# Fewer transposes on TensorE, and the order of a hand-planned attention and MLP kernel searched anew

## The chip, the cores and the metric

The kernel runs on one core of one Trainium2 chip. The metric is device time in microseconds (us), as a median of runs. TensorE (PE) multiplies, VectorE (DVE) and ScalarE (ACT) work element by element and take results out of PSUM, GpSimd (POOL) here issues the loads that change float32 into bfloat16, and SyncE (SP) issues DMA transposes and stores.

## The reference

Attention without softmax and with a decay per head, then an MLP with exact GELU over all tokens:

```
q, k, v: (8, 8, 576, 64)                       # batch, heads, sequence, head size
gamma = 1 - 2 ** (-5 - head)
D[i, j] = gamma ** (i - j) if i >= j else 0
attn = ((q @ k.T) / 8 * D) @ v                 # per batch and head
x = attn as (4608, 512)                        # tokens, heads * head size
out = gelu(x @ w_in) @ w_out                   # w_in (512, 2048), w_out (2048, 512)
```

## The kernel before

**Units, pairs and blocks.** The sequence of 576 is cut into chunks of 128 (the last, a tail, has 64). A unit is 128 tokens: one chunk of one batch entry, or the tails of two. There are 36 units. Batch entries go two by two; a pair is the same chunk of two entries. Units 0 to 3 (two pairs) come first, then 4 and 5, 6 and 7, 8 and 9 (the fifth pair), the tail 10, 11 and 12, and so on. Four units make a block of 512 tokens for the MLP, and there are nine blocks, t = 0 to 8.

**Attention of a unit.** q, k and v land in bfloat16. Then q and k are turned, so that the head size lies on partitions: for units below `N_PE_TR` by TensorE (`turn`, four products against the identity for q and four for k, into the PSUM tile `qk_ps`, copied to `qkT` by `turned_copy` on VectorE or ScalarE), for the others by one DMA transpose for q and one for k of a whole pair, issued on SP (`turn_dma`, L613). `scores` multiplies k with q (PSUM tile `sc`), VectorE multiplies by the decay (L657, `ret`), `inner` multiplies by v (`o_ps`), and `cross` adds what older chunks leave in a state `u`, which `state` collects in `u_ps` from k and the scaled values `vh`. `vh` of a unit is one VectorE instruction, or eight ScalarE instructions where the unit is in `VH_ACT` (L829). The result is copied or scaled into `xT` of its block.

**MLP of a block.** The first product (`hT`) is followed by a GELU on ScalarE. For blocks 0 and 1 it is plain: block 1 in two halves of 256 tokens; in block 0 the eight pairs of 128 hidden columns that `WIDE` lists are multiplied with 512 tokens at once, after those that it does not list, which are multiplied with 128 tokens (one unit) at a time, as `CUTS` has it:

```
if t == 0: cuts of 128 tokens, m in K_ORDER[::2] if m not in WIDE
then       [("1", t, m + n, 1, 0, TOK) for m in WIDE for n in range(2)]
```

The pieces of that second list run in the order of the list. From block 2 on, groups of hidden columns are either plain ("p3") or go by a fast scheme of seven products ("units" `yT`, `zT`, `xT_`, with sums `xs` of x and `wi_sum` of the weights). `LAYOUTS` says which group of a block goes how and in which order; "01" weaves the products of two groups, "0", "1" runs them one after the other, "2p3" weaves a fast with a plain one. The second product (`oT`) is plain for block 0 and fast from block 1 on, in the order `SECOND`; results go to `o_sb` and are stored from SP, the last block's from ScalarE's queue as well.

**What sets the order.** While the program is built, a planner with an estimated length for every operation simulates the engines and emits instructions in the order in which they would start. The order on each engine is thus fixed in the built program, and each engine runs its own in order. Loads are issued on GpSimd in the sequence `ORDER` (q1 is q of unit 1; wi3 and wo3 are the fourth of eight pieces of w_in and w_out; `pos` is a small table), at most eight in flight, from unit 11 on in the order of the units, with four buffers for pairs. Attention's products are put between the MLP's as short stretches; `need`, made of `LEAD` and `SPREAD`, and `SHIFT`, `APART`, `BEFORE`, `GAP_A`, `HOLD`, `LOOK` and `EASE` set when and in which grouping. In its first 16 us the planner fills each pause of TensorE with products of zeros (`warm`), 512 columns wide or 128, that nobody reads.

Of the kernel before, what the change touches and what calls it, by code (L numbers as in the profile page):

```python
# [29 lines left out]
class Plan:  # L30
# [9 lines left out]
    def add(self, name, engine, dur, deps, fn, due=0.0, lag=0.12, **more):  # L40
        assert name not in self.ops, name
        op = self.ops[name] = Op(name, engine, dur, deps, fn, due, lag, **more)
        for d in op.deps:
            if d.startswith("land"):
                self.users.setdefault(d, []).append(op)
            dep = self.ops.get(d)
            if dep is None or dep.end is None:
                op.waits += 1
                self.later.setdefault(d, []).append(op)
            else:  # L50
                op.ready = max(op.ready, dep.end + dep.lag)
        if not op.waits:
            self.released(op)
        return op
# [53 lines left out]
def kernel(  # L108
# [47 lines left out]
    def pair_with(i):  # L156

        bp, ci, j = units[i]
        return [i] if j is None else pair_of[bp, ci]

    def slot_of(i):
        return pair_with(i)[0]
# [2 lines left out]
    n = v_order.index(pair_of[1, 1][0])  # L165
    v_order[n:n] = kept

    N_PE_TR = 10
    N_LD = 4
    N_QKT = 4  # L170
    N_VH = 5
    N_RET = 3
    N_Q = 4
    VH_ACT = [5, 6, 7, 8, 9, 10, 21, 22, 23, 24, 26, 27, 28, 29, 30, 31, 33, 34, 35]
    HOT = 10.1
    N_WARM = 8
    SLACK = 0.2
    CUTS = (0, 128, 256, 384, 512)
    AHEAD = 6
    WIDE = [2, 10, 14, 12, 4]  # L180
    VH_DUE = 14.0
    PARTS = 4
    FAST = 1
    FETCH = 4.0
    BUSY_FETCH = 6.2
    GAP_A = 4.7
    GAP_B = 0
    SHIFT = {4: -0.5, 5: 4.0, 6: 4.5, 7: -2.0, 8: 6.0, 9: 0.5, 10: 0.5, 11: -6.0, 12: -3.5, 13: -0.5, 14: -3.5, 15: -0.5, 16: -4.5, 17: -2.0, 18: -3.5, 19: 0.0, 20: 1.0}
    APART = [3, 5, 6, 7]
    BEFORE = 8.1  # L190
    UNIT_FROM = 2
    LOOK = 12
    HOLD = 6
    LAYOUTS = {2: ['01', '2', 'p3'], 3: ['01', '2', 'p3'], 4: ['1', '02', 'p3'], 5: ['0', '1', '2', 'p3'], 6: ['01', '23'], 7: ['01', '23'], 8: ['0', '12', 'p3']}
    LEAD = 8.9
    SPREAD = 5.6
    EASE = 9
    ORDER = ("k2 k1 pos q1 wi0 q3 k3 q2 v1 v2 v3 wi4 wi7 wi1 wi5 v4 k4 q5 wi6 k5 wi3 wi2 q4 wo0 v5 wo4 wo1 q9 wo5 "
             "q8 v7 wo6 v6 q7 q6 wo2 k7 v10 wo7 wo3 k6 q10 k8 v8 k10 k9 v9").split()
    K_ORDER = [0, 1, 8, 9, 2, 3, 10, 11, 4, 5, 12, 13, 6, 7, 14, 15]  # L200
    PRODUCTS = "3251467"
    SECOND = "1267534"
# [1 line left out]
    for t in range(UNIT_FROM, N_BLK):  # L204
        LAYOUT[t] = LAYOUTS[t]

# [99 lines left out]
    for t in range(N_BLK):  # L306
        if t < 2:
            cuts = CUTS if t == 0 else (0, 256, 512)
            for lo, hi in zip(cuts, cuts[1:]):
                stream.append([("1", t, m, 2, lo, hi) for m in K_ORDER[::2] if t or m not in WIDE])  # L310
            if t == 0:
                stream.append([("1", t, m + n, 1, 0, TOK) for m in WIDE for n in range(2)])
        else:
# [44 lines left out]
    pos = const.tile([128, 1, NCI], FP32, name="pos")  # L358
# [121 lines left out]
    def tiles_of(i):  # L480

        if i not in loaded:
            n = slot_of(i)
            if i in kept:
                loaded[i] = (const.tile([128, 2, H, D], BF16, name=f"qk_ld{i}"), const.tile([128, H, D], BF16, name=f"v_ld{i}"))
                return loaded[i]
            if n not in slots:
                ld_ring.take()
                slots[n] = (ld_pool.tile([128, 2, H, 2, D], BF16, tag="qk", name="qk_ld"),
                            ld_pool.tile([128, 2, H, D], BF16, tag="v", name="v_ld"))  # L490
            qk, v_ld = slots[n]
            j = units[i][2] or 0
            if i in old:
                loaded[i] = (qk.rearrange("p a (j h) b d -> p j a (h b) d", j=2)[:, j], v_ld[:, j])
            else:
                loaded[i] = (qk[:, :, :, j], v_ld[:, j])
        return loaded[i]

    def read(i, what):
# [4 lines left out]
        want = {(m, x) for m in pair_with(i) for x in  # L504
                ["v"] + (["turn0", "turn1"] if i < N_PE_TR else ["turn"]) + (["state"] if units[i][1] < NCI - 1 else []) + (["inner"] if i in raw else [])}
        if i not in kept and want <= got:
# [33 lines left out]
    for i in range(11, N_U):  # L540
        ORDER += [f"{what}{i}" for what in "qkv"]
    prev = ["val"]
    for item in ORDER:
        what = item.rstrip("0123456789")
# [77 lines left out]
    def scores(i):  # L622
        if i in old:
            qkT = qkT_of(i)
            got = [bank([128, HP, 128], FP32, f"sc{e}") for e in range(2)]
            for hp in range(HP):
                for e in range(2):
                    sl = slice(64 * e, 64 * e + 64)
                    product(got[e][1][:, hp, :], lhsT=qkT[sl, 1, hp, :], rhs=qkT[sl, 0, hp, :],
                                     start=True, stop=True)  # L630
        else:
            qkT, n = qkT_of(i), i - slot_of(i)
            got = [bank([128, HP, 128], FP32, f"sc{e}") for e in range(2)]
            for hh in range(HP):
                h = 4 * n + hh
                for half in range(2):
                    out_ = slice(64 * half, 64 * half + 64)
                    for e in range(2):
                        sl = slice(64 * e, 64 * e + 64)
                        product(got[e][1][out_, hh, :], lhsT=qkT[sl, 1, h, out_], rhs=qkT[sl, 0, h, :],  # L640
                                         start=True, stop=True)
        st[i]["sc"] = got
# [225 lines left out]
    for n, g in enumerate(groups):  # L868
        need[n] = begins["1", g[0] // 4] - LEAD
    for n in reversed(range(len(groups) - 1)):  # L870
        need[n] = min(need[n], need[n + 1] - SPREAD)
    tiles_of(0)
# [5 lines left out]
    EARLY = 3  # L878
    ALONE = [groups[n][0] for n in range(2, len(groups)) if n in APART or groups[n - 1][0] not in fine]
    for i in range(N_U):  # L880
# [4 lines left out]
        room_T = lambda i=i: 0.0 if slot_of(i) in turned_of else tr_ring.at()  # L885
        if i < N_PE_TR:
            for jj, nm in enumerate("qk"):
# [7 lines left out]
        if i not in fine and i not in tails:  # L895
            add(f"scores{i}", "pe", 0.23, [f"T{i}.0", f"T{i}.1"] if i < N_PE_TR else [f"landT{m}" for m in duo],
                lambda i=i: scores(i), due, DRAIN, banks=2, mode="row" if i in old else "quad")
# [16 lines left out]
        if i > n:  # L914
            continue
        Ts = [f"T{m}.{jj}" for m in duo for jj in range(2)] if n < N_PE_TR else [f"landT{m}" for m in duo]
        if n in ALONE:
# [15 lines left out]
    for i in v_order:  # L933
        due = need[group_of[i]] + 3.0 if i not in kept else need[group_of[pair_of[1, 1][0]]] - 2.0
        n = v_order.index(i)
        room = lambda i=i, due=due: max(0.0 if "vh" in st[i] else vh_ring.at(), due - EASE if group_of[i] > 3 else 0.0)
        before = ["dv", f"land v{i}"] + ([f"vh{v_order[n - 1]}"] if n else [])
        if i in VH_ACT:
            step_ = H // PARTS
# [472 lines left out]
    def macro_of(n):  # L1412


        back, front = groups[n - 1], groups[n] if n < len(groups) and n not in APART else []
        states = states_behind(n - 1)
# [12 lines left out]
    def scores_of(front):  # L1429
        return [f"both_{i}" if i in fine or i in tails else f"scores{i}" for i in front if i not in fine or i == slot_of(i)]  # L1430

    def states_behind(n):

        if n < 0:
            return []
        i = groups[n][0]
        bp, ci, j = units[i]
        if j is None:
            return [(1, 0)] if bp == 0 else []
        return [] if (bp, ci) == (1, 0) else [(bp, ci)]  # L1440
# [3 lines left out]
    for n in range(EARLY + 1, len(groups) + 1):  # L1444
        macros += [(n, names, need[n - 1] + SHIFT[n]) for names in macro_of(n)]
        if n in APART:
            macros.append((n, scores_of(groups[n]), need[n] - BEFORE))
    in_macro = {nm for m in macros for nm in m[1]}
# [98 lines left out]
    def pe_candidates():  # L1547
# [7 lines left out]
        if macros and not got:  # L1555
            ahead = next((W[r[0]] for r in heads if r), NEVER)
            n, ops, due = macros[0]
            hold = ahead >= due + HOLD and (macro_start(ops, False) or NEVER) <= T["pe"] + 0.3
        for run in heads:
# [4 lines left out]
            else:  # L1564
                look = run[:LOOK]
            for one in look:
# [7 lines left out]
        if macros and not any(g[1] == 0 for g in got):  # L1574
            n, ops, due = macros[0]
            at = macro_start(ops)
            if at is not None:
                at = max(at, stretch_end[0] + (GAP_B if ops[0].startswith("in_b") else GAP_A))
                ahead = next((W[r[0]] for r in heads if r), NEVER)
# [10 lines left out]
    while True:  # L1590
# [12 lines left out]
        if e == "pe":  # L1603
# [9 lines left out]
            else:  # L1613
                for run in heads:
                    got = [one for one in run[:LOOK] if f"mlp{one}" == op.name]
                    if got:
# [46 lines left out]
```

## Time and profile before

| | us |
|---|---|
| median of 3 runs | 280.59 (280.51 to 280.66) |
| the profiled execution | 281.12 |
| its span, first to last instruction | 279.2 |
| TensorE busy | 273.0 (98%), 3626 products |
| VectorE, ScalarE, GpSimd busy | 228.7, 181.7, 110.4 |
| granted TensorE clock | 1.000 |

The profile is of one execution. Matmuls are pipelined and their ends are modelled, so busy TensorE time says little; the distance from the start of one product to that of the next says what it costs. A landing is the time at which the last part of a DMA's data has arrived.

### The profile page before, as it was taken

Reading aid. Unit: us, or ns where it says so; the run is one execution under the profiler, and the core shown is the slowest. Engines: PE = TensorE matmul, PEld = TensorE weight load, DVE = VectorE, ACT = ScalarE, POOL = GpSimd, SP = SyncE. Lnnn points to the kernel's source line nnn. Section 1 sums busy time; section 2 is a strip of 40 time slices with the busy share of each in tenths; the row PEclk is TensorE's granted clock in tenths of the full one; section 3 lists DMA queues with packets and bytes.
Section 4 is the critical chain, followed back from the end, with each engine's and each line's share of the span. In section 5 each row is a group of like instructions: output and inputs, shape, how many; then the busy total and the mean of one; then the engine's idle time right before and its main releaser. Section 6 shows DMA issues by size and latency. Waiting matters only on the chain.

```text
span 279.2 us, 8727 instructions
## 1 busy us (share of the span) xinstructions
PE 273.0 (98%) x3626; PEld 216.2 (77%) x3626; DVE 228.7 (82%) x437; ACT 181.7 (65%) x446; POOL 110.4 (40%) x139
## 2 busy tenths in 40 slices
PE   7999999999999999999999999999999999999995
PEld 2675567478888688868886888778888888888684
DVE  5862554589989997999898999997899979969843
ACT  7766638786418823693559657975896689627840
POOL 8977688809755097311452725705000000000000
PEclk9999999999999999999999999999999999999999
DMA  9999999999999999999999999999600040003013
GB/s 150 161 187 179 190 175 173 178 169 165 149 142 177 193 134 151 134 236 99 142 197 88 128 160 222 116 113 121 190 2 2 6 151 2 2 22 131 0 40 113
DMA packets 152374, 35.55 MB, mean 127 GB/s; under 512 B 141072, under 2 KB 148240, under 8 KB 152336
## 3 DMA queue, kind: packets, MB, share of 16 engines
q0 software_dynamic: 115792, 17.97, 97.6%
q1 hardware_dynamic: 34544, 15.93, 31.0%
q10 hardware_dynamic: 2000, 1.11, 1.4%
q8 instruction: 28, 0.46, 0.7%
q14 instruction: 10, 0.08, 0.1%
HBM read 36.70 MB, written 9.44 MB: 165 GB/s over the span
## 4 chain that ended last, share of the span: by engine, by line
PE 79%; DMA 14%; POOL 5%; issue 1%; ACT 0%; DVE 0%; POOLq 0%
PE oT L231 37%; PE zT L231 11%; PE hT L231 9%; DMA w_out<-in_moe_w_out_dram 9%; PE yT L231 7%; PE o_ps L231 4%; DMA w_in<-in_moe_w_in_dram 3%; PE sc L231 2%; POOL qk_ld L522 2%; DMA qk_ld<-in_k_dram 2%; PE u_ps L231 2%; POOL w_in L528 1%; POOL v_ld L522 1%; PE xT__1851 L231 0%; PE xT__5150 L231 0%
## 5 line engine op out<-in xcount | busy, mean ns | idle before, releaser
L231 PEld LDWEIGHTS <-g 128*128 128x128 bf16 x576 | 55.2, 98 | 12.5 <-issue 0.4
L231 PEld LDWEIGHTS <-w_in 128*128 128x128 bf16 x528 | 47.2, 98 | 15.9
L231 PEld LDWEIGHTS <-wi_sum 128*128 128x128 bf16 x460 | 44.6, 98 | 7.1 <-issue 0.4
L231 PE MATMUL hT<-xT,w_in 128*128 128x256 bf16 (+2 forms) x344 | 49.0, 295 | 0.0
L231 PE MATMUL oT<-w_out,g 128*128 128x256 bf16 (+1 forms) x320 | 45.6, 294 | 0.1
L522 POOL DMA_DIRECT2D qk_ld<-in_q_dram x31 | 27.8, 898 | 38.9 <-DMA qkT<-qk_ld 24.2
L829 ACT ACTIVATE vh<-v_ld,dv 128x64 bf16<-128x64 bf16 x152 | 41.3, 348 | 1.0 <-DVE ret L657 1.0
L231 PEld LDWEIGHTS <-s 128*128 128x128 bf16 x384 | 36.8, 98 | 5.3 <-issue 0.4
L1104 ACT ACTIVATE g<-hT 128x512 bf16<-128x512 f32 (+1 forms) x58 | 31.5, 558 | 11.1 <-PE hT L231 10.4
L522 POOL DMA_DIRECT2D v_ld<-in_v_dram x31 | 28.0, 906 | 14.0 <-issue 6.7
L231 PE MATMUL oT<-w_sum,s 128*128 128x256 bf16 x256 | 32.6, 273 | 0.3 <-issue 0.3
L231 PE MATMUL oT<-w_sum,g 128*128 128x256 bf16 x256 | 31.1, 273 | 0.0
L1248 ACT COPY o_sb<-oT 128x512 f32<-128x512 f32 (+1 forms) x27 | 14.3, 539 | 23.7 <-PE oT L231 12.1
L522 POOL DMA_DIRECT2D qk_ld<-in_k_dram x31 | 28.0, 905 | 2.8 <-DMA v_ld<-in_v_dram 1.4
L1217 ACT ACTIVATE g<-zT 128x512 bf16<-128x512 f32 x46 | 26.4, 608 | 0.7 <-DVE zT L1226 0.6
L657 DVE TENSOR_TENSOR ret<-sc,msk 128x512 bf16<-128x512 f32 x36 | 22.9, 683 | 4.3 <-PE sc L231 4.3
L1252 DVE TENSOR_TENSOR o_sb<-o_sb,oT 128x512 f32<-128x512 f32 (+1 forms) x27 | 16.6, 626 | 10.5 <-PE oT L231 5.7
L834 ACT CAST u_sb<-u_ps 128x512 bf16<-128x512 f32 x19 | 11.3, 596 | 14.4 <-PE u_ps L231 12.5
L860 DVE TENSOR_TENSOR xT<-o_ps,dqT 128x512 bf16<-128x512 f32 x26 | 17.1, 683 | 1.9 <-PE o_ps L231 1.9
L573 DVE COPY qkT<-qk_ps 128x512 bf16<-128x512 bf16 x16 | 6.4, 421 | 13.9 <-PE qk_ps L235 13.8
L1226 DVE TENSOR_TENSOR zT<-q,zT 128x512 f32<-128x512 f32 x23 | 15.8, 692 | 2.1 <-PE zT L231 1.8
L575 ACT COPY q<-yT 128x512 f32<-128x512 f32 x16 | 9.0, 600 | 11.7 <-PE yT L231 11.7
(173 smaller groups left out, 470.6 us busy)
## 6 DMA issues: line engine op xcount, KB each, us to landing
out_dram<-o_sb SPq DMA_DIRECT2D x29, 256.0 KB, 3.4
qk_ld<-in_k_dram POOLq DMA_DIRECT2D x31, 128.0 KB, 7.2
qk_ld<-in_q_dram POOLq DMA_DIRECT2D x31, 128.0 KB, 7.5
v_ld<-in_v_dram POOLq DMA_DIRECT2D x31, 128.0 KB, 7.8
w_in<-in_moe_w_in_dram POOLq DMA_DIRECT2D x8, 256.0 KB, 8.1
w_out<-in_moe_w_out_dram POOLq DMA_DIRECT2D x8, 256.0 KB, 8.4
out_dram<-o_sb SPq DMA_DIRECT2D x7, 128.0 KB, 2.4
out_dram<-o_sb ACTq DMA_DIRECT2D x5, 128.0 KB, 1.9
```

The source lines that it names most:

```text
L231: return nc.tensor.matmul(*args, **more)
L522: nc.gpsimd.dma_start(dst, src[2 * bp + j, :, ci * C:ci * C + C, :].rearrange("h s d -> s h d"))
L575: nc.scalar.copy(dst, src)
L657: nc.vector.tensor_tensor(r, t, by, op=ALU.mult)
L829: nc.scalar.activation(vh[:, h], loaded[i][1][:, h], AF.Copy, scale=dv[:, h, ci:ci + 1])
L834: ins = (nc.vector.tensor_copy if engine == "dve" else nc.scalar.copy)(u_sb[t if bp >= FINE else ci % 2], u_bank[1])
L860: nc.vector.tensor_tensor(dst, o, dqT[:, :, ci * C:ci * C + C], op=ALU.mult)
L1104: nc.scalar.activation(g_of(t, m0)[:, m0 % 2:m0 % 2 + n, m0 // 8, lo:hi], hT, AF.Gelu)
L1217: nc.scalar.activation(target(key, what), chain[key][n][1], AF.Gelu)
L1226: nc.vector.tensor_tensor(to, chain[key]["q"], z, op=ALU.add)
L1248: nc.scalar.copy(target(key, what), chain[key][n][1])
L1252: nc.vector.tensor_tensor(to, to, chain[key][n][1], op=ALU.add)
```

## The change

`N_PE_TR` goes from 10 to 8, so units 8 and 9 are turned by two DMA transposes on SP and no longer by 16 products on TensorE with four copies. `WIDE` lists all eight pairs of block 0, so nothing of it is multiplied by units any more. `VH_ACT` gives 14 units to ScalarE where it gave 19 (36 and 37 are no units). The loads have a new `ORDER`, blocks 3, 5, 6, 7 and 8 a new layout, and several constants and the shifts of the planner's placing are others. No line of a function changes.

```
-    N_PE_TR = 10
+    N_PE_TR = 8
-    VH_ACT = [5, 6, 7, 8, 9, 10, 21, 22, 23, 24, 26, 27, 28, 29, 30, 31, 33, 34, 35]
+    VH_ACT = [4, 5, 6, 7, 10, 11, 15, 16, 20, 21, 22, 23, 31, 33, 36, 37]
-    WIDE = [2, 10, 14, 12, 4]
+    WIDE = [6, 8, 10, 14, 0, 4, 2, 12]
-    GAP_A = 4.7
+    GAP_A = 2.3
-    SHIFT = {4: -0.5, 5: 4.0, 6: 4.5, 7: -2.0, 8: 6.0, 9: 0.5, 10: 0.5, 11: -6.0, 12: -3.5, 13: -0.5, 14: -3.5, 15: -0.5, 16: -4.5, 17: -2.0, 18: -3.5, 19: 0.0, 20: 1.0}
-    APART = [3, 5, 6, 7]
-    BEFORE = 8.1
+    SHIFT = {4: -2.0, 5: -6.5, 6: -4.0, 7: -5.0, 8: 4.5, 9: 5.0, 10: -2.0, 11: 0.0, 12: 1.0, 13: -1.5, 14: -2.5, 15: 2.5, 16: 0.0, 17: -3.5, 18: 1.0, 19: 3.0, 20: 2.5}
+    APART = [4, 6, 7]
+    BEFORE = 0.7
-    LOOK = 12
-    HOLD = 6
-    LAYOUTS = {2: ['01', '2', 'p3'], 3: ['01', '2', 'p3'], 4: ['1', '02', 'p3'], 5: ['0', '1', '2', 'p3'], 6: ['01', '23'], 7: ['01', '23'], 8: ['0', '12', 'p3']}
-    LEAD = 8.9
-    SPREAD = 5.6
-    EASE = 9
-    ORDER = ("k2 k1 pos q1 wi0 q3 k3 q2 v1 v2 v3 wi4 wi7 wi1 wi5 v4 k4 q5 wi6 k5 wi3 wi2 q4 wo0 v5 wo4 wo1 q9 wo5 "
-             "q8 v7 wo6 v6 q7 q6 wo2 k7 v10 wo7 wo3 k6 q10 k8 v8 k10 k9 v9").split()
+    LOOK = 17
+    HOLD = 4.2
+    LAYOUTS = {2: ['01', '2', 'p3'], 3: ['01', '2p3'], 4: ['1', '02', 'p3'], 5: ['01', '2', 'p3'], 6: ['10', '23'], 7: ['0', '1', '23'], 8: ['3', '20', 'p1']}
+    LEAD = 8
+    SPREAD = 7.9
+    EASE = 7.1
+    ORDER = ("pos q1 k2 q2 v2 v3 wi0 q3 k3 k1 v1 wi4 wi3 wi7 k5 wi5 wi1 v4 q4 k4 wi2 q9 v5 q5 wo5 wi6 wo0 wo1 wo4 "
+             "q6 k7 q8 v10 v6 v7 wo2 wo6 wo3 wo7 k6 k9 q10 q7 k10 k8 v8 v9").split()
```

In the built program TensorE has 3551 products where it had 3626: 64 transposes (80), 144 products of hT with 512 columns and none with 128 (120 and 96), 43 warming products (30), all else in the same numbers. SP issues 32 DMA transposes (30).

## The prediction

> **What bounds the kernel now.** I read the page first (engine shares, slices), then TensorE's row of the chain of waits, then the order of time of the first 32 us, then the landings of single loads.
>
> ```profile
> span 279.2 us, 8727 instructions
> PE 273.0 (98%) x3626; PEld 216.2 (77%) x3626; DVE 228.7 (82%) x437; ACT 181.7 (65%) x446; POOL 110.4 (40%) x139
> PE   7999999999999999999999999999999999999995
> PEclk9999999999999999999999999999999999999999
> ```
>
> TensorE is busy in every slice but the first and the last. What it waits for, by the waits view of TensorE alone:
>
> ```profile
> PE warm L231 <- DVE ln_scale L352: 1.2, 1, 1.2
> PE qk_ps L235 <- DMA qk_ld<-in_k_dram: 0.7, 1, 0.7
> PE oT L231 <- issue: 0.3, 1, 0.3
> PE zT L231 <- ACT g L1217: 0.2, 1, 0.2
> ```
>
> Ends are modelled there; from start to start, the pauses after 17 us that are no change of tile shape are 0.30 us (at 32.7), 0.84 (52.9, the second row), 0.43 (108.4, the third) and 0.38 (171.4, the fourth): 1.94 us in all. The last product starts at 275.7, the span ends 3.5 us later. So time can come from three places only: fewer or cheaper products, fewer than 1.94 us of waits, or an earlier start of the useful work. The third is the order of time of the first stage (start, duration, what):
>
> ```profile
> 13.81 2.72 DVE L657 TENSOR_TENSOR ret<-sc,near 128x512 bf16<-128x512 f32 x4
> 16.23 0.74 PE L231 MATMUL o_ps<-ret,v_ld 128*64 128x128 bf16 x16
> 16.45 0.68 DVE L826 TENSOR_TENSOR vh<-v_ld,dv 128x512 bf16<-128x512 bf16 x1
> 16.68 1.07 ACT L575 CAST xT<-o_ps 128x512 bf16<-128x512 f32 x2 [0.61 <-PE o_ps L231]
> 16.90 0.62 PE L231 MATMUL hT<-xT,w_in 128*128 128x128 bf16 x8
> 17.45 0.44 PE L231 MATMUL u_ps<-vh,qk_ld 128*64 128x64 bf16 x16
> ...
> 26.11 0.61 PE L235 MATMUL qk_ps<-ident,qk_ld 128*128 128x128 bf16 x8
> 26.56 3.68 PE L231 MATMUL hT<-xT,w_in 128*128 128x512 bf16 x40
> ```
>
> Four masks take 2.72 us (0.68 each), two copies to xT 1.07. Eight transposes start 0.45 us ahead of what follows: 0.056 each. With 128 columns a product of hT also takes 0.056; with 512 it takes 0.216 (28 of them fill the 6.05 us from 20.06 to 26.11). The first hT products run before all four units of block 0 are ready, because three of eight weight pairs are cut by units.
>
> **What the change removes.** 16 transposes on TensorE: 16 x 0.056 = 0.9 us, on the path, and four copies of 0.42 us that lay beside it. Instead, SP issues two whole DMA transposes more.
>
> A rule of the Trainium skill would make this gain larger. "TensorE: Matmul & The Clock Gate", Part 4, puts a 128x128 transpose at about 275 ns in a kernel and says the fast clock does not engage in it; by that, 16 would save 4.4 us. The row above (0.056 us each) contradicts it, and the row decides; the 278.9 that the rule would give gets no chance.
>
> **What it does to the start.** All eight pairs are now in WIDE, so no hT product of block 0 can start before x of units 0 to 3 is whole; and the new ORDER loads k1 ninth (it was second). The first ten loads are the same ten in both orders and GpSimd issues one each 0.9 us, so places keep their landings. Place 9 is v2 in the trace: issue 8.5, landing 6.2 us later; place 12 (the weights that the new order needs first, wi3) is issued at 11.0:
>
> ```profile
> DMA to landing us min/median/max: 6.2/6.2/6.2
> ...
> DMA to landing us min/median/max: 7.9/7.9/7.9
> ```
>
> So k1 lands at 14.65 and wi3 at 18.8. Behind k1, by rows: transposes until 15.1; its copy, which the built order gives to ScalarE, 0.59, to 15.7; scores, seen by VectorE at 16.2; then three masks in a row on VectorE, 3 x 0.68, to 18.25 (the fourth, of unit 3, stands first and is done by 16.0); vh of unit 1, 0.68, to 18.95; o_ps of unit 3, 0.35, and its copy to xT by 19.3; u_ps until 19.4. The first hT product starts at 19.45. Eleven more of the warming products fill the gap and do nothing. By 19.45 the kernel before had run 16 + 8 + 28 narrow hT products, 52 x 0.056 = 2.9 us.
>
> **The sum.** From 19.45 to the last product's start at 275.70 the kernel before needs 256.25 us, 1.94 of it waits: 254.3 of work. The new one adds the 52 narrow products as 13 wide ones, 13 x 0.216 = 2.8; saves 0.9 (transposes) and 0.1 (the 44 later narrow products as 11 wide ones). The attention products stand in 31 stretches where 29 stood; most are the same, but one of 80 products (1.62 us) becomes 48 + 32 (1.17 + 0.57) and one of 32 is split, and each change to or from such a stretch costs 0.09: +0.3 together. That makes 256.4, so 275.85 with no wait at all: already 0.15 later than now. New waits come on top.
>
> **New waits.** (1) Units 6 and 7 are now turned late: q7 is load 42, which landed at 51.55, and the added q transpose of units 8 and 9 runs before it in the same stretch of time. Alone, a whole DMA transpose took 3.2 us from issue to landing (186.91), beside loads up to 11.4 (119.69). How much of that the loads lose is not seen: nothing at best, 3.2 us each at worst; I take 1 to 2, as loads that landed 0.85 apart stood 2.1 to 2.3 apart beside the transposes at 52 us. The second group of transposes is reached at 52.5 by adding up rows, so it waits 0 to 2 us: 0.6. (2) The first units of block 2 start 0.9 us after the attention stretch ahead of them, where 1.3 lay between; xT and xs (two of 0.64, one of 0.41 on VectorE) need 1.9 before the first yT: 0.5. (3) LAYOUTS runs units 0 and 1 of block 7 one after the other, as block 5 did where the 0.38 us pause was: 0.4, while block 5 loses its own. (4) vh of units 4 and 5 both go to ScalarE between gelus (16 x 0.25 + 8 x 0.6 us), done at 34.0 where u_ps wants them at 34.0: 0.2. Sum 1.7, so the last product starts at 277.55, 1.85 us later. The tail of 3.5 us is untouched (SECOND, the stores and PARTS stay). The profiled execution was 281.12 us, its span 279.2; it stands 0.5 above the median of 280.59. The shift of 1.85 applies to both: 282.4.
>
> **Costed at nothing.** Five of nineteen vh move from ScalarE to VectorE (36 and 37 in the list are no units): 5 x 0.68 = 3.4 us more on VectorE, less 1.7 for the copies. VectorE is busy 19.5 of 20 us from 60 to 100, but there two come (8, 9) and three go (11, 15, 16). The cover is attention's lead; without it 0.68 us each. On SP the first added transpose waits for q8 (about 39) with nothing behind it until the stores at 51; the second waits for k8 (about 54) and holds two stores of block 0 behind it, whose buffer ScalarE needs next: no one waits within 5 us.
>
> **Rivals.** *Loads fall behind* (12%). Loads wait for slots, and three of them waited 24.2 us in all for transposes to land ("POOL qk_ld L522 <- DMA qkT<-qk_ld", longest 10.3). Smallest slack in the trace between such a landing and its scores: 71.62 to 77.34, 5.7 us. Two more transposes ahead, each up to 3.2, and the same contention for the loads would use it up; beyond that each us is paid: some 3 us more, 285.4. *Same* (17%): the start as computed, the waits at 0 to 0.4: 280.7 to 281.1. *Faster* (10%): the start itself. If the first wide product starts at 17.8 (as the steady hT does now) and no wait replaces the 1.94, the last product starts at 275.85 - 1.65 = 274.2: 279.1. It decides from a start before 18.7 without waits, before 17.0 with the waits above. For it: eight wide warming products (1.7 us) stand between the scores and the last o_ps, which suits an o_ps at about 17.9. Against it: three masks and vh stand behind k1's scores on VectorE, and wi3 lands at 18.8 whatever they do. *Clock* (2%): TensorE is mostly idle or warming from 16.2 to 19.4; if the slow start (0.64 us per wide product until 6.3) came back for 3 us, 1.5 to 2 us are added: 284.2. The page named above says in Part 1 that an idle window of some 3.4 us brings half the clock back; the granted clock reads 1.0 throughout, even over that slow start. That the change does not do what it says is excluded: the built order has 64 transposes, 144 wide hT products and 32 DMA transposes.
>
> **How the numbers follow.** The forecast has 59%. What a measurement can tell from no change is 0.2%, 0.56 us. Faster holds its rival's 10%, same its 17%, slower the rest, 73%. The range goes from no wait, 0.1 better start (280.5), to the loads falling behind (285.2).
>
> **What would show it.** First wide hT at 19.4 or later, with VectorE's masks until 18.2; TensorE's work after it 0.1 longer than now; a pause at the second group of transposes of units 6 and 7 at 52.5 to 54; no pause at 56 to 77 on scores. Wrong: a first hT before 18.5, or waits under 0.4 us in all.

## The result and the profile after

| | before | after |
|---|---|---|
| median | 280.62 (280.51 to 280.97, 4 runs) | 284.01 (283.73 to 284.75, 4 runs) |
| the profiled execution | 281.12 | 284.01 |
| its span | 279.2 | 282.1 |
| first hT product of any width starts | 11.46 | 19.67 |
| first wide hT product starts | 20.07 | 19.67 |
| last product starts | 275.70 | 277.95 |
| from there to the end of the span | 3.5 | 4.15 |

The ratio is 1.0118 (95%: 1.01 to 1.0137). In the second timing of the same kernel (e8 below) it is 1.0141 (1.0121 to 1.0161). The change makes the kernel 3.4 us slower in the first timing and 3.9 in the second. The ratios leave out two executions that stood over 1.5% above the fastest of their kernel, one of e1 (302.4 us) and one of e6 (286.8), while the medians hold them. The forecast was 282.4 in a range of 280.5 to 285.2, with 0.73 for slower.

The page of after, the lines that answer to those of before:

```profile
span 282.1 us, 8534 instructions
PE 275.6 (98%) x3551; PEld 213.1 (76%) x3551; DVE 229.2 (81%) x438; ACT 171.3 (61%) x400; POOL 110.4 (39%) x139
PE   7999999999999999999999999999999999999994
PEclk9999999999999999999999999999999999999999
```

There are 75 products fewer on TensorE, and it is busy 2.6 us longer. The 96 narrow hT products became 24 wide ones that take as long together, and the 52 of them that had filled the time before 19.5 gave way there to 13 more warming products, 11 of them wide (about 2.5 us), which nobody reads. The clock is full throughout. What TensorE waits for, by the waits view of TensorE alone (us in total, times, longest):

```profile
PE warm L231 <- DVE ln_scale L352: 1.2, 1, 1.2
PE hT L231 <- ACT xT L575: 0.4, 1, 0.4
PE zT L231 <- ACT g L1217: 0.3, 1, 0.3
```

The wait for k9 (0.7) is gone, and the first hT product waits for x. The order of time of the first stage (start, duration, what, in brackets the idle time before):

```profile
15.60 2.65 DVE L657 TENSOR_TENSOR ret<-sc,near 128x512 bf16<-128x512 f32 x4 [0.37 <-PE sc L231]
16.26 1.90 PE L231 MATMUL warm<-u_sb 128*128 128x512 bf16 x8
18.09 0.64 PE L231 MATMUL o_ps<-ret,v_ld 128*64 128x128 bf16 x16
18.17 0.68 DVE L826 TENSOR_TENSOR vh<-v_ld,dv 128x512 bf16<-128x512 bf16 x1
18.55 1.07 ACT L575 CAST xT<-o_ps 128x512 bf16<-128x512 f32 x2 [2.85 <-PE o_ps L231]
18.56 0.75 PE L231 MATMUL u_ps<-vh,qk_ld 128*64 128x64 bf16 x16
19.67 3.61 PE L231 MATMUL hT<-xT,w_in 128*128 128x512 bf16 x16 [0.36 <-ACT xT L575]
```

Four masks stand in a row on VectorE until 18.25, then o_ps, then two copies on ScalarE until 19.62, then the first wide product. Before 19.67 nothing of the MLP is done. The chain starts with k1 (ninth load, issued at 8.38, landed at 14.63), by the view of that line:

```profile
L522 POOL DMA_DIRECT2D qk_ld<-in_k_dram x1: 942/942/942, 8.4 to 8.4; - x1
...
DMA to landing us min/median/max: 6.2/6.2/6.2
```

The tail is new. Of ScalarE's six last stores, the second and third by the view of the store's line (min/median/max in ns), first before, then after:

```profile
L1305 ACTq DMA_DIRECT2D out_dram<-o_sb x2: 595/598/601, 273.1 to 273.8; - x2
```

```profile
L1305 ACTq DMA_DIRECT2D out_dram<-o_sb x2: 605/1091/1577, 275.4 to 276.0; - x2
```

The third store takes 1.58 us to issue, not 0.60, and the rest stand behind it: ScalarE's sixth store lands 3.14 us behind the start of the last product, where in before the last landing, of a store from SP, came 2.51 behind it. That is the 0.65 by which the span ends later than the last product explains. The first two stores, issued at 274.77 and 275.36, already take 3.5 and 3.1 us to land (2.0 and 2.1 in before), so not only the issue is held up. In the DMA view of after from 275 to 277 us there is one packet that isn't data:

```profile
q10 hardware_dynamic: 144, 0.12, 27.2%
q8 instruction: 1, 0.02, 4.7%
```

So 2.25 us come before the last product and 0.65 behind it: 2.9 in the span. The median moved by 3.4, because the profiled execution of before stood 0.5 above its median and that of after stands on it.

### The profile page after: what moved, and what is told of

The parts are those of the page before. It is cut to its first block, busy times and chain, and to the rows that moved or that the text cites. A ratio compares the mean times of both kernels' runs of the same rounds, so it can differ in the third digit from the quotient of the medians.

```text
span 282.1 us, 8534 instructions
## 1 busy us (share of the span) xinstructions
PE 275.6 (98%) x3551; PEld 213.1 (76%) x3551; DVE 229.2 (81%) x438; ACT 171.3 (61%) x400; POOL 110.4 (39%) x139
## 4 chain that ended last, share of the span: by engine, by line
PE 93%; DVE 4%; ACT 1%; issue 1%; DVEq 0%
PE oT L231 39%; PE hT L231 16%; PE zT L231 10%; PE yT L231 6%; PE o_ps L231 4%; PE warm L231 4%; PE sc L231 3%; PE qk_ps L235 2%; PE u_ps L231 2%; DVE o_sb L1252 1%; DVE ret L657 1%; ACT g L1217 1%; DVE xs L1059 1%; DVE xT L860 0%; ACT xT L575 0%
## 5 line engine op out<-in xcount | busy, mean ns | idle before, releaser
L231 PEld LDWEIGHTS <-w_in 128*128 128x128 bf16 x456 | 44.2, 98 | 18.8 <-issue 0.3
L231 PE MATMUL hT<-xT,w_in 128*128 128x512 bf16 (+1 forms) x272 | 49.2, 329 | 0.4 <-ACT xT L575 0.4
L231 PE MATMUL oT<-w_out,g 128*128 128x256 bf16 (+1 forms) x320 | 46.3, 294 | 0.1
L1104 ACT ACTIVATE g<-hT 128x512 bf16<-128x512 f32 x52 | 30.5, 601 | 10.7 <-PE hT L231 10.0
L522 POOL DMA_DIRECT2D v_ld<-in_v_dram x31 | 27.9, 901 | 16.4 <-DVE vh L826 6.9
L829 ACT ACTIVATE vh<-v_ld,dv 128x64 bf16<-128x64 bf16 x112 | 31.0, 344 | 5.3 <-DMA v_ld<-in_v_dram 5.3
L1252 DVE TENSOR_TENSOR o_sb<-o_sb,oT 128x512 f32<-128x512 f32 (+1 forms) x27 | 16.8, 625 | 7.9 <-PE oT L231 3.9
L575 ACT COPY q<-yT 128x512 f32<-128x512 f32 x20 | 11.2, 595 | 19.0 <-PE yT L231 18.9
L860 DVE TENSOR_TENSOR xT<-o_ps,dqT 128x512 bf16<-128x512 f32 x26 | 16.8, 683 | 2.6 <-PE o_ps L231 2.6
L573 DVE COPY qkT<-qk_ps 128x512 bf16<-128x512 bf16 x14 | 5.5, 421 | 15.9 <-PE qk_ps L235 15.9
L834 ACT CAST u_sb<-u_ps 128x512 bf16<-128x512 f32 x18 | 10.6, 591 | 11.2 <-PE u_ps L231 9.3
```

What stands on the lines that cost most here:

```text
L231: return nc.tensor.matmul(*args, **more)
L522: nc.gpsimd.dma_start(dst, src[2 * bp + j, :, ci * C:ci * C + C, :].rearrange("h s d -> s h d"))
L575: nc.scalar.copy(dst, src)
L829: nc.scalar.activation(vh[:, h], loaded[i][1][:, h], AF.Copy, scale=dv[:, h, ci:ci + 1])
L834: ins = (nc.vector.tensor_copy if engine == "dve" else nc.scalar.copy)(u_sb[t if bp >= FINE else ci % 2], u_bank[1])
L860: nc.vector.tensor_tensor(dst, o, dqT[:, :, ci * C:ci * C + C], op=ALU.mult)
```

## The experiments

Times are medians; the kernel before had 280.99 beside e1 to e7, 280.58 beside e8 and e9, 280.93 beside e10 and e11, and 281.02 beside e12.

**e1: the transposes alone, in the kernel before.**

```
-    N_PE_TR = 10
+    N_PE_TR = 8
```

> The kernel before with N_PE_TR = 8 and nothing else changed (the planner places the rest anew). The start is the same, instruction by instruction. Theory (the loss is the start, the transposes are a gain): 16 x 0.056 = 0.9 us less on TensorE and about a switch of shape less, so 279.5 to 280.0 against 280.6. Rival (two more DMA transposes hold the loads back and TensorE waits for scores): 281 or more, with a pause at a stretch of scores between 50 and 80 us.

Measured: 299.2, ratio 1.0644 (1.0608 to 1.0679). The theory falls; the rival has the sign, but the loss is far larger than it says. From the order of time on TensorE:

```profile
58.47 0.42 PE L231 MATMUL u_ps<-vh,qk_ld 128*64 128x64 bf16 x16
66.97 1.07 PE L231 MATMUL sc<-qkT 64*64 64x128 bf16 x32 [8.09 <-DMA qkT<-qk_ld]
67.83 0.64 PE L231 MATMUL o_ps<-qkT,u_sb 64*64 64x128 bf16 x16
69.86 6.32 PE L231 MATMUL hT<-xT,w_in 128*128 128x256 bf16 x30 [1.39 <-DVE xT L860]
```

The transpose of k of units 8 and 9 is issued at 58.23 and lands at 66.93; TensorE stands for it 8.25 us, counted from start to start as all pauses below. The windows of the same stretch (span, length, busy time of each engine, granted clock, DMA share, GB/s) show a second price:

```profile
61.00:62.00 1.00, 0.00 (x0) 0.00 (x0) 1.00 (x4) 1.00 (x6) 0.00 (x0) 1.00 1.40 252
62.00:63.00 1.00, 0.00 (x0) 0.00 (x0) 1.00 (x4) 0.49 (x2) 0.58 (x1) 0.55 2.19 172
67.00:68.00 1.00, 1.00 (x40) 1.00 (x44) 0.34 (x1) 0.00 (x0) 1.00 (x2) 0.50 1.48 289
75.00:76.00 1.00, 1.00 (x7) 0.76 (x6) 0.00 (x0) 0.60 (x1) 0.71 (x1) 0.62 2.21 151
76.00:77.00 1.00, 1.00 (x12) 0.88 (x10) 0.00 (x0) 0.57 (x1) 0.32 (x1) 1.00 2.44 155
```

A mean of 0.55 from 62 to 63 puts the fall of the clock at 62.1, 3.2 us after the modelled end of the last product (58.9) and 3.4 after its start (58.69); 0.62 from 75 to 76 puts its return at 75.8. Of the 8.8 us from 66.97 to there 1.65 are a pause, so 7.1 us of work ran at half clock, 3.6 us lost. With the pauses of 8.25, 1.65, 1.38 (at 49.95), 0.86 (85.8) and 0.49 (106) that makes 16.2 us; smaller pauses add some 3, and before's 1.94 of pauses and the 0.9 of the transposes come off. That leaves about 16.4 of the 16.8 us by which the last product starts later. The Trainium skill, "TensorE: Matmul & The Clock Gate", Part 1, gives an idle window of about 3.4 us for the fall to half clock; this trace agrees, with its 3.2 to 3.4. What follows: N_PE_TR = 8 needs another place for the scores of units 8 and 9, and the new order has it. There they run at 68.81, not 56, and the landing is at 67.77: 1.0 us of slack.

**e2: the old WIDE in the kernel after.**

```
-    WIDE = [6, 8, 10, 14, 0, 4, 2, 12]
+    WIDE = [2, 10, 14, 12, 4]
```

> The changed kernel with the old WIDE = [2, 10, 14, 12, 4]: block 0's other three pairs are again multiplied unit by unit, all else as changed. Theory (start): x of units 0 and 2 is ready by 14, so most of the 2.9 us of narrow products fit in ahead of 19.7 in place of warming products: 281.0 to 282.0 against 284.0. Rival (waits and layouts later on cost it): 283.5 to 284.3.

Measured: 289.85, ratio 1.0309 (1.0273 to 1.0346). The theory falls. The start is as early as it says (first hT product at 12.15), but later waits outweigh it, some of them for loads that the new order brings late. TensorE's waits, the view cut to what is new (the profiled execution, 291.89, is the slowest of the six):

```profile
PE oT L231 <- issue: 3.6, 4, 2.4
...
PE qk_ps L235 <- DMA qk_ld<-in_k_dram: 1.2, 1, 1.2
PE hT L231 <- DMA w_in<-in_moe_w_in_dram: 1.1, 3, 0.7
PE hT L231 <- DVE xT L860: 1.0, 1, 1.0
PE qk_ps L235 <- DMA qk_ld<-in_q_dram: 0.9, 1, 0.9
```

Work done early is given back, and more, in waits for weights, q, k and x and, the largest, in four waits for "issue" (more on these at the end). In this run the old start does not fit the rest of the new order; that the search fitted the order to a late start is argued, not shown.

**e3: k1 early in the kernel after** (the first ten loads in nearly the old places).

```
-    ORDER = ("pos q1 k2 q2 v2 v3 wi0 q3 k3 k1 v1 wi4 wi3 wi7 ...
+    ORDER = ("pos q1 k1 k2 q2 v1 v2 q3 k3 v3 wi0 wi4 wi3 wi7 ...
```

> The changed kernel with k1 as second load and v1 as fifth (the first ten loads are the same ten); all of block 0 stays 512 wide. Theory (the chain behind k1 sets the first wide product): x is whole about 2 us earlier, wi3 lands at 17.8, so the first wide product moves from 19.7 to about 18 and the time from 284.0 to about 282.3. Rival (something else than k1 sets the start, or the start does not matter): 283.5 to 284.3.

Measured: 287.03, ratio 1.0232 (1.0208 to 1.0256). The theory falls: x is whole at 19.23, only 0.4 us sooner than in after, because unit 3 now comes last (k3 landed at 13.98, its mask ends at 17.73, its o_ps starts at 18.19, its copy to xT at 18.64). The product then waits for its weights (wi3, landed at 19.33) and starts at 19.38, 0.3 us sooner:

```profile
19.38 1.90 PE L231 MATMUL hT<-xT,w_in 128*128 128x512 bf16 x8 [0.77 <-DMA w_in<-in_moe_w_in_dram]
```

So the chain of k3 and the weights stand close behind k1's chain and take its place. Later waits of TensorE, 0.49 for w_out, 1.01 for k, 1.42 for x and 0.54 for a transpose, add 3 us: here a part of the order could not be moved without loss in the rest.

**e4: the new start in the kernel before** (WIDE and ORDER of after, all else old, ten units turned on TensorE).

```
-    WIDE = [2, 10, 14, 12, 4]
+    WIDE = [6, 8, 10, 14, 0, 4, 2, 12]
-    ORDER = ("k2 k1 pos q1 wi0 q3 k3 ...
+    ORDER = ("pos q1 k2 q2 v2 v3 wi0 ...
```

> The kernel before with WIDE and ORDER of the changed one: the first 123 products up to the first hT are those of the changed kernel; transposes, layouts and shifts are the old ones. Theory (start): first hT at 19.7 and 2.9 us of work not done before it, so about 283.3 against 280.6, which with the 0.9 of the transposes is more than the changed kernel loses without its own waits. Rival: 280.3 to 281.3.

Measured: 283.14, ratio 1.0079 (1.0067 to 1.0092). The rival is excluded, and the theory holds in its time, though the loss is 2.15 us against 280.99 where it has 2.7. The new start with its loads costs about two thirds of what the whole change costs; e6 below has a late start without them. The first wide product starts at 19.79, the last product at 277.49, 1.8 us later than before:

```profile
19.79 7.93 PE L231 MATMUL hT<-xT,w_in 128*128 128x512 bf16 x35 [0.36 <-ACT xT L575]
```

Of before's 1.94 us of pauses 0.25 (at 39.6), 0.13 and 0.10 are left.

**e5: two DMA transposes more, nothing else.** The kernel before, instruction for instruction; SP turns q and k of units 8 and 9 a second time, into a tile that nobody reads.

```
...
+                nc.sync.dma_start(spare[:, :, :], slots[8][0][:, jj_].rearrange("p h b d -> p (h b d)"), transpose=True)
...
```

> The kernel before, instruction for instruction on every engine, with two more DMA transposes on SP: q and k of units 8 and 9, as soon as they have landed, into a tile that nobody reads (TensorE still turns these units). This prices the two DMA transposes by themselves, with no one waiting for their result. Theory (the loads lose 1 to 2 us to each, and TensorE's wait for k9 at 52.9 grows by that): 0.5 to 2 us more than before, 281.2 to 282.7, with the later stages unchanged in shape. Rival (loads fall behind for good, slots and all): 3 us more or above.

Measured: 283.49, ratio 1.0085 (1.0059 to 1.011); 2.5 us more, between the theory's 2 at most and the rival's 3 at least; the last product starts 2.8 us later. The wait for k9, which the theory would have grow, shrank: TensorE, late itself, stood 0.50 us at 55.4 until k9 had landed (55.79), where it was 0.84 in before. The two transposes are issued at 37.64 and 55.85 and land 8.5 and 10.3 us later. TensorE's waits:

```profile
PE oT L231 <- DMA w_out<-in_moe_w_out_dram: 1.8, 1, 1.8
...
PE sc L231 <- DMA qkT<-qk_ld: 1.0, 1, 1.0
PE qk_ps L235 <- DMA qk_ld<-in_q_dram: 0.5, 2, 0.3
```

A piece of w_out is late behind the first, a transpose of other units behind the second. No engine but SP and the DMA had more to do, so the two transposes have a price of their own: 2.8 us here, three times what 16 transposes on TensorE take. Not all of it is time that the loads lose: SP's issues stand in a fixed order too. Its stores of block 0 came 2.3 us later than in before, it then stood 1.5 us (54.35 to 55.85) for k9, and the issue of the second took 1.5 more, so the transposes behind it were issued at 57.52 and 59.78, not at 52.14 and 53.88. The two parts were not told apart.

**e6: the old kernel, 2.8 us later.** Thirteen wide products of zeros, unread, ahead of the last o_ps of block 0, all else instruction for instruction.

```
...
+                for _ in range(13):
+                    nc.tensor.matmul(t_, lhsT=zeros[:, :128], rhs=zeros, start=True, stop=True)
...
```

> The kernel before, instruction for instruction, with 13 more products of zeros (512 columns, 2.8 us) on TensorE ahead of the last o_ps of units 1 and 3 at 16.2. This prices the late start by itself. Theory (TensorE is the bound, so a late start goes to the end, less the waits that it hides): 2.8 us later at 19.7, of which up to 1.6 come back as the waits for k9, w_out and the like vanish: 281.8 to 283.4. Rival (landings of the loads set the pace up to 54 us, the start is free): 280.6 to 281.1.

Measured: 283.5, ratio 1.0078 (1.0051 to 1.0105), as the theory has it. The order of time shows the products put in:

```profile
16.12 2.97 PE L1609 MATMUL warm<-u_sb 128*128 128x512 bf16 x13
```

The last product starts 1.92 us later, for 2.8 us put in: 0.9 us are taken out of old waits, as loads and transposes gain a lead (the pauses for w_out and k9, 0.30 and 0.84, are gone). That is the size of e4's loss, with no change of order at all.

**e7: ten units on TensorE again, in the kernel after.**

```
-    N_PE_TR = 8
+    N_PE_TR = 10
```

> The changed kernel with N_PE_TR = 10 again: TensorE turns units 8 and 9, everything else as changed (the planner places the rest anew; the start is the same). Theory (16 transposes cost 0.9 us on TensorE, the DMA transposes have cost little in the new order): 284.6 to 285.2 against 284.0. Rival (the two DMA transposes cost more than they save): 283.5 or less.

Measured: 285.24, ratio 1.015 (1.0122 to 1.0178) against 1.0118 of after: 0.9 us more, as the theory has it, but the intervals overlap, and beside the second timing of after (e8, 1.0141) next to nothing is left. The times don't settle it; the traces do. The last product starts at 279.08, 1.13 later than in the first profile of after, with one new wait of 0.3 to 0.5 at 79 us. From the first wide product to the last product, less the pauses of 0.1 and more, e7 needs 257.7 us, and after 256.8 in both of its profiles. So 16 transposes cost 0.9 us, 0.056 each. The figure weighed in the prediction (the Trainium skill, "TensorE: Matmul & The Clock Gate", Part 4: about 275 ns each) would make it 4.4 us; the runs disagree with it as a cost. As the duration of a single one it is near to what the trace of before shows, 241 ns on average with modelled ends: the transposes overlap, and the distance from start to start is what they cost.

**e8: the kernel after once more.**

> The changed kernel itself once more, profiled anew. What is open: its profile ended 4.15 us after the last product's start, where the kernel before and all seven other experiments ended 3.4 to 3.5 us after it, with the ScalarE queue's six stores taking 4.32 us from first to last against 3.57. Theory: nothing of the change reaches the tail (the last stores, their pieces and their queues are the same), so the long tail was one execution's own; then this profile has its last product's start at 277.9 to 278.1 again, a tail of 3.4 to 3.6, and a span of 281.4 to 281.6; the median is 283.4 to 284.0. Rival: a later order of the last stage's work makes the stores collide, so the tail is 4.0 or more again and the span 282.0 or more.

Measured: 284.45, span 283.5 in its profile. The theory falls: the tail is about 4.15 again, and the third store takes 1.47 us. It is no chance of one execution. The last product starts at 279.33, though, 1.4 later than in the first profile, and the pauses at 52.8 and 81.0 are now 0.69 and 0.57 (0.11 and 0.11 in the first):

```profile
53.74 0.45 PE L235 MATMUL qk_ps<-ident,qk_ld 128*128 128x128 bf16 x5 [0.53 <-DMA qk_ld<-in_q_dram]
```

That is q7, landed at 53.69 (52.76 in the first profile).

**e9: k9 ahead of k10 in the kernel before.** The first idea for a faster kernel: its largest pause, 0.84 us, waits for k9.

```
-                nc.gpsimd.dma_start(dst, src[2 * bp + jj, :, ci * C:S, :].rearrange("h s d -> s h d"))
+                if (what, i) == ("k", 10):
+                    later.append(...)
...
+        if (what, i) == ("k", 9):
+            for one in later:
+                nc.gpsimd.dma_start(*one)
```

> The kernel before, instruction for instruction, but the two small loads of k10 (a tail unit's, not needed before 60) are issued behind the load of k9, not ahead of it. In the trace of before TensorE waited 0.84 us at 52.87 for k9, which landed at 53.79; k10 was issued at 46.27 and k9 at 48.04. Theory (TensorE's waits sit on the path, so one that is removed comes off the end): k9 is issued 1.4 to 1.8 us sooner and lands at 52.4 to 53.2, the pause falls to 0.0 to 0.3, and the last product starts 0.5 to 0.8 us sooner, at 274.9 to 275.2: 280.2 to 280.5 against 281.0. Rival (a load's landing is set by what the queue carries, not by its place, or other waits take over what is saved): the pause stays at 0.6 or more, or later pauses grow by as much, and the time is 280.8 to 281.1. This is also a try at a faster kernel: the theory that added waits are partly hidden by a later start says that waits which are removed can bring out later ones.

Measured: 280.07 in a spread of 279.94 to 284.02, ratio 1.0002 (0.9977 to 1.0027). In the profile k9 lands at 52.28, the pause is gone, and the last product starts at 274.44. The time doesn't settle it.

**e10: TensorE's instructions counted otherwise, in the kernel after.**

```
-            product(t[:, :n], lhsT=zeros[:, :128], rhs=zeros[:, :n], start=True, stop=True)
+            if n == 512 and 16.0 <= T["pe"] < 18.0:
+                made[0] += 1
+                for _ in range(4):
+                    nc.tensor.matmul(t[:, :128], lhsT=zeros[:, :128], rhs=zeros[:, :128], start=True, stop=True)
...
```

> The changed kernel, order and layouts untouched, but seven of the eight wide warming products ahead of the last o_ps (512 columns each, their result unread) are each given as four of 128 columns: the same time on TensorE (0.056 against 0.216), 42 TensorE instructions more (21 weight loads, 21 products). What is open: the tail of 4.15 to 4.17 us in both profiles of the changed kernel, where all others have 3.4 to 3.5. In both, the third of ScalarE's six last stores took 1.58 and 1.47 us to issue (0.60 elsewhere), and one packet of 0.02 MB of an instruction queue (28 packets in the span, 0.46 MB, which is 64 bytes for each of some 7100 TensorE instructions) lies at 275.5 to 276.0, between the first and the third store; in the kernel before the last such packet lies 14 us ahead of the end, in two experiments with 32 instructions more 8 us. Theory: that packet, TensorE's own instruction load, holds up the store, and its place is set by the number of TensorE instructions. 42 more of 0.055 us each put it 2.3 us earlier, at 273.2 to 273.8, ahead of the first store (274.8): the store takes 0.6, the tail is 3.4 to 3.6, and the span 281.3 to 281.6: 0.6 us less than the changed kernel. Rival: the store's delay comes from the last stage's order, which this leaves alone: the tail stays at 4.1 or more.

Measured: 285.32 (283.37 to 286.75), span 283.7. On the tail the theory holds: the packet is at 275 to 276, ahead of the first store (277.17), and the same two stores take

```profile
L1305 ACTq DMA_DIRECT2D out_dram<-o_sb x2: 596/600/605, 277.8 to 278.4; - x2
```

with a tail of 3.35. The span it forecast doesn't come, and the median is no lower than after's, because there are other waits; this execution has one that neither profile of after has:

```profile
81.78 0.64 PE L231 MATMUL sc<-qkT 64*64 64x128 bf16 x32 [1.82 <-DMA qkT<-qk_ld]
```

The second transpose of units 11 and 12 took 11.4 us from issue to landing; in the first profile of after it took 8.7 and landed 2.3 us ahead of its scores. The new order leaves little slack at 52.8, 68.8 and 80; that the runs spread by it is likely, but only three executions were profiled. Whether the edit itself had a part in the wait is open.

**e11: e9 again.**

> The kernel before with k9 loaded ahead of k10, once more, because its first timing spread from 279.94 to 284.02 and its interval holds no change. Theory (a wait that is removed comes off the end): 280.0 to 280.5, 0.1 to 0.2% under the kernel before, with the pause of 0.84 at 52.9 gone. Rival (the gain lies in one profiled execution only): 280.6 to 281.0.

Measured: 280.38 (279.97 to 281.68), ratio 0.9986 (0.9966 to 1.0006). Seven of the twelve times lie at 279.97 to 280.65, five at 281.13 to 281.68. This profile, of the second group, has one pause more:

```profile
107.66 0.28 PE L231 MATMUL oT<-w_sum,s 128*128 128x256 bf16 x1
108.85 0.92 PE L231 MATMUL oT<-w_sum,s 128*128 128x256 bf16 x7 [0.90 <-issue]
```

Its instruction packet lies between 106 and 107; in e9's profile, without the pause, it lies between 102 and 104. The pause of 0.43 at 108.4 in the kernel before stands at the same product, with its packet between 106 and 107 too.

**e12: e9 with 54 TensorE instructions more** (9 wide warming products as four narrow ones each, as in e10).

> The kernel before with k9 loaded ahead of k10, and 9 wide warming products before 18 us each given as four of 128 columns (54 TensorE instructions more, the same time on TensorE, their result unread). What is open: the two timings of the k9 kernel fall in two groups, near 280.05 and near 281.1; the profile of one near 281.1 has a pause of 1.08 us after the first oT product behind the attention stretch at 107.7, which waits for nothing but issue, and its packet of TensorE's instruction queue lies at 106 to 107; the profile of one at 279.94 has no pause there and its packet lies at 102 to 104. Theory: TensorE waits there for the next block of its own instructions, 256 to a block. With 54 more ahead, the block's edge comes 27 pairs of weight load and product earlier, inside the attention stretch: no pause after that first oT product (under 0.1), and if the block is late again, 0.3 to 1.3 us somewhere among the attention products of 106.2 to 107.6. The time is 280.0 to 280.3 if it is in time, 281.0 to 281.5 if it isn't. Rival: the pause belongs to the oT product (a buffer, VectorE behind), so where the packet is at 105 to 107 it is seen after the same first product, 0.3 to 1.1 us. Neither says which of the two times is the commoner.

Measured: 280.74 (280.02 to 282.32), ratio 0.9997 (0.9978 to 1.0016). The profiled execution has its packet at 102 to 104 and no pause, so where the block's edge lies was not told apart. A faster kernel is not shown: the medians of e9, e11 and e12 are 0.5, 0.55 and 0.3 under before's, and each interval holds 1.

## Why the prediction was right

The direction was right, and so was the mechanism of the start; the size was not: the forecast has the kernel 1.85 us slower, little more than half of the 3.4 measured. Term by term:

**The start.** It forecast k1 at 14.65, masks until 18.25 and the first wide product at 19.45; they came at 14.63, 18.25 and 19.67. The last copy to xT, forecast for 19.3, ended at 19.62, as the two copies stand one behind the other on ScalarE. The weights wi3, forecast for 18.8, landed at 17.81; in e3, from the same place in the queue with wi0 later ahead of them, at 19.33. e4 and e6 show the term in the sum: +1.8 and +1.9 at the last product.

**The sum of products.** Forecast from the first wide product to the last product with no wait: 256.4 us. Measured: 277.95 less 19.67, less pauses of 1.45 (those of 0.1 and more): 256.8. The 0.9 of the transposes is what e7 shows. The regrouping is the term that came out too small: e4, in the old grouping and with ten units turned on TensorE, needs 257.2, only 0.4 more than after, so that about 0.5 is left for the regrouping where 0.3 was forecast.

**The waits.** Forecast 1.7 us; 1.45 in the first profile of after and 2.6 in the second. That the sum falls between them is partly luck, for the places are half right. Block 2's start paused 0.48 at 89.98 (forecast 0.5), though for ScalarE's GELU and not for VectorE's sums; block 7's separate units paused 0.16 (forecast 0.4). The second group of units 6 and 7 paused 0.11 in one execution and 0.69 in the other (forecast 0.6). vh of units 4 and 5 cost nothing (forecast 0.2). Not forecast are 0.27 at 128.3 and three of 0.11 to 0.17.

**The tail.** "The tail of 3.5 us is untouched" is the step that failed: 4.15, the last stores meeting an instruction block. With the start's 0.2 and the 0.4 of products, less 0.25 of waits, it is most of what the forecast of 282.4 lacked; the rest is the 0.5 that the profile of before stands above its median, which the forecast gave to the kernel after as well.

**Costed at nothing.** The second added transpose was to have 5 us of lead before anyone waits. It was issued at 57.39, not 54, behind two of unit 10 (53.18 and 55.26) on the same queue, landed at 67.77, and had 1.0 us before its scores. e1 shows what it costs where that lead is gone, 8.25 us and the clock with it. *Loads fall behind* was priced at 3 us: e5, with 2.8, is that rival in the old order. In the new one it is avoided, since the scores come 12 us later, but not by much (e10).

**Rivals.** *Faster* needed a start before 18.7; excluded by the rows above. *Same* needed waits of 0 to 0.4, and there were 1.45. *Clock*: granted 1.0 from 14 to 24 us in after, with pauses of 0.3 and 0.36 there, far from the 3.2 us of e1. The prediction also reads 1.0 over the slow first 6 us; the clock's records in that trace begin at 9.9 us, so this reading says nothing.

**The range.** Its ends don't follow from the terms: no wait and a start 0.1 better give 280.6, not 280.5, and the rival's 285.4 lies above the upper end of 285.2.

The whole closes for the first profile: from e4 to after the start is 0.1 earlier, the work 0.4 less (the transposes' 0.9, less 0.5 of regrouping), and the waits 1.0 more, so 277.49 becomes 277.95 up to rounding. The late start is the loss, and the transposes' gain goes into regrouping and waits.

## What to carry to other kernels

Work on the bound engine that fills the wait for the first data is free, and moving it behind that wait costs its whole length; only the part that later waits would have taken anyway (0.9 of 2.8 us here) comes back. A step moved from the bound engine to the DMA is free only if its consumer moves back with it and if loads in the same stretch can spare the time: price both, the landing beside loads and the loads beside it. Where an order was searched as a whole, parts of it set back alone (e1, e2, e3) measure how they fit the rest, not what they are worth.

## What the runs showed of the hardware

Instructions come by DMA and get in the way of stores. One instruction queue moves 28 packets, 0.46 MB, in the span: 16 KB each, or, shared among TensorE's 7102 instructions (products and weight loads), about 65 bytes each; that the queue is TensorE's is taken from this count. In after one packet lies among the last stores, one of which then takes 1.58 us to issue (1.47 in e8) instead of 0.60; 42 TensorE instructions more took the packet out of their way (e10), though the median didn't fall. It is not peculiar to the tail: in the fourteen traces 26 stores took over 0.8 us to issue, and 16 of them start within 0.75 us behind the start of such a packet; of the 604 shorter ones 11 do. Waits "for issue" go with such packets too: after the first 20 us there are seven over 0.4 us from start to start, and each begins 0.8 to 2.1 us behind a packet, beside running DMA transposes; the longest are 2.6 at 80.4 in e2 (packet at 79.6) and 1.1 at 107.7 in e11 (106.1). That TensorE waited there for its instructions is argued from place and packet; it was not shown, as e12 did not hit the case. The Trainium skill, "Runtime: NRT & Kernel Launch", section "Instruction fetch mechanics", has blocks of 16 KiB, which agrees, and calls the cost of crossing from one to the next mostly hidden; here one cost 0.65 us at the tail.

The clock went down and up in steps of one length in e1: the trace records full clock for 51.2 us up to 62.11, half clock for 13.65 us up to 75.76, and full clock again; that is 15 and 4 times 3.41 us. In the last 3.41 us before the fall TensorE started nothing, and the last 3.41 us before the return are the first such step after the stall in which it had no pause. One run shows this, so it is an inference.

Until 106 us, beside loads, a DMA transpose of q or k of a pair took 7.7 to 13.3 us from issue to landing in the two profiles of after, where 3.2 were seen alone; the same one (k of units 11 and 12) took 8.7 there and 11.4 in e10.
